# Loading q and k of the first two batches as a casting DMA in 1.5 KB runs, in GpSimd's queue, beside plain loads in SyncE's

## The chip, the cores and the metric

The kernel runs on one core of a Trainium2 chip. The metric is the device time of one execution in microseconds. Five engines run side by side, each through its own queue of instructions in program order: TensorE (PE; its weight loads are the row PEld), VectorE (DVE), ScalarE (ACT), GpSimd (POOL) and SyncE (SP). DMAs are issued from such a queue too; SP issues most of them here, and POOL issues those that change the type on the way. All of them are carried by the same 16 DMA engines.

## The reference

Sliding-window attention with a linear distance bias, followed by one feed-forward layer:

```python
# q, k, v: (8 batches, 8 heads, 576 tokens, 64), float32
scores = q @ k.T / sqrt(64)                      # per batch and head
mask   = (rel >= 0) & (rel < 128)                # rel = query - key
scores = where(mask, scores - slope[h] * abs(rel), -1e9)
attn   = softmax(scores) @ v
x      = attn.transpose(0, 2, 1, 3).reshape(4608, 512)
h      = x @ w_in                                # (512, 2048)
out    = (h * clip(h + 3, 0, 6) / 6) @ w_out     # (2048, 512)
```

## The kernel before

**Attention.** The unit of work is a pair of heads, `g` = 0 to 31: pair `g` belongs to batch `g // 4`. A pair's q and k are needed transposed, with the 64 dimensions on the partitions: two heads fill 128. `scores` (line 186) multiplies blocks of 128 keys by the same block of queries (`scd`) and by the next one (`sco`). `exp_diag` and `exp_off` take the exponential on ACT, and POOL masks the result in place (lines 216, 228, 232). `values` (line 236) multiplies by v, which carries a column of ones for the sums, in two calls, one for three blocks of queries and one for two; DVE divides. `back` (line 264) writes the result transposed into `xT`: on PE and DVE for the last pair and for batches below `NB_PE`, by a transposing DMA (an "xbar") from SP for the others.

**Loading.** q, k and v arrive as float32 in four rotating buffers. A row of `load_tokens` (line 97) brings a batch's q, k or v in five DMAs, one for each block of tokens; every packet is the 256 bytes of one token of one head. Batch 0 comes in the finer order of `load_pair`. From there q and k go one of two ways. In batch 0, `prepare` casts a pair on DVE, and `transposes` turns it on PE, five blocks each for q and k, with copies out of PSUM on DVE and ACT. In all later batches, `cast_tokens` casts the whole batch on POOL into `qbuf` or `kbuf`, and `xbar` (line 156) turns it by one DMA from SP into `qTb` or `kTb`. v is cast on POOL always. The two weights are loaded and cast to bfloat16 by POOL's DMAs, in 2 KB packets, w_in after pair 0 and w_out after pair 7.

**Feed-forward.** `units` (line 318) lists 288 units of four matmuls of 512 columns: `moe_up` (L284, then ACT L288 and DVE L289) and `moe_down` (L301). `fill(n)` writes the next n units into the program, unless the next one is a `moe_up` whose 512 tokens (one "nt") are not all done: `done` counts the pairs whose result is in `xT`. nt 0 needs batch 0, nt 1 needs batch 1, nt 2 needs batch 2.

**Order.** All engines run in the order in which the program is written. `first_batch` does pairs 0 to 3 without units. After it come seven units, and `segment` takes pairs 4 to 31 in loops: scores of `g`, exponentials of `g`, values of `g - 1`, with units between them by a table of seven places (two in a loop of batch 1, eight from batch 2 on). At the end of a loop `stage_next` issues casts, xbars and loads for later batches. So a cast on POOL, which waits for a load or a buffer, stands ahead of the next pair's masks, and an xbar in SP's queue stands behind the loads issued before it.

## Time and profile before

| | us |
|---|---|
| median of 3 runs | 395.62 (395.07 to 396.06) |
| profiled execution | 395.14 |
| its span, first to last instruction | 393.4 |
| PE busy | 311.4 (79%) |
| ACT, DVE, POOL busy | 199.0, 164.3, 151.3 |
| mean granted TensorE clock | 0.939 |

The span is cut into 40 slices of 9.8 us on the page. Views used below are the slices, the list of who waited for whom, the groups of instructions by line, the timeline of one engine, windows of chosen length, and the instructions of one tile. In a timeline a row is start, duration, engine, line, operation, output and inputs, and how many were merged; in square brackets stands the idle time ahead of it and what ended it. `SPq` is SP issuing DMAs.

### The profile page before, as it was taken

The numbers are of one execution on the slowest core, as the hardware profiler recorded it, in microseconds if no ns is written. First come the engines' busy times: TensorE is split into PE (matmuls) and PEld (weight loads), VectorE is DVE, ScalarE is ACT, GpSimd is POOL, SyncE is SP. The second block draws the span as 40 slices with busy tenths as digits, with TensorE's granted clock in tenths as the row PEclk, the third lists the DMA queues.
The fourth block names the chain that finished last, engine by engine and source line by source line (L and its number), as shares of the span: only waits on it lengthen the run. The fifth ranks groups of instructions, "written<-read, shape, count | busy, mean of one in ns | idle before, by whom it ended". The sixth has DMA issues, their size and how long they took to land.

```text
span 393.4 us, 6368 instructions
## 1 busy us (share of the span) xinstructions
PE 311.4 (79%) x2334; PEld 156.3 (40%) x2369; DVE 164.3 (42%) x348; ACT 199.0 (51%) x365; POOL 151.3 (38%) x246
## 2 busy tenths in 40 slices
PE   2577407600458989998999899899999999999985
PEld 1354103300324544554454455454554444444432
DVE  5654402510126534544554455455545544344420
ACT  2653306810327754675776567576677533444410
POOL 1684405980232665555467455536224100000000
PEclk9999957955659999999999999999999999999999
DMA  7999999899994996999699799952121101001012
GB/s 159 219 196 203 200 215 214 153 160 192 202 163 97 223 223 144 205 198 211 148 211 238 131 221 214 220 112 57 48 71 45 46 27 53 28 27 55 27 53 80
DMA packets 176718, 55.95 MB, mean 142 GB/s; under 512 B 167856, under 2 KB 172208, under 8 KB 176688
## 3 DMA queue, kind: packets, MB, share of 16 engines
q1 hardware_dynamic: 172320, 51.23, 69.2%
q0 software_dynamic: 4224, 4.19, 6.7%
q8 instruction: 18, 0.29, 0.3%
q10 hardware_dynamic: 144, 0.13, 0.1%
q14 instruction: 12, 0.10, 0.1%
HBM read 36.70 MB, written 9.44 MB: 117 GB/s over the span
## 4 chain that ended last, share of the span: by engine, by line
PE 59%; SPq 20%; DMA 8%; ACT 3%; issue 3%; POOL 3%; DVE 2%; POOLq 0%
PE ops L301 28%; PE hps L284 25%; SPq L101 14%; DMA xT<-avs 4%; SPq L90 3%; DMA ld_v<-in_v_dram 3%; SPq L158 2%; ACT r L288 2%; PE av L249 2%; PE scd L193 2%; DMA ld_q<-in_q_dram 1%; PE av L246 1%; DVE osb L315 1%; DVE g L289 1%; POOL pd L216 1%
## 5 line engine op out<-in xcount | busy, mean ns | idle before, releaser
L289 DVE SCALAR_TENSOR_TENSOR g<-r,hps 128x512 bf16<-128x512 f32 x144 | 99.0, 688 | 188.0 <-ACT r L288 187.9
L288 ACT ACTIVATE r<-hps,bias 128x512 f32<-128x512 f32 x144 | 99.7, 692 | 140.8 <-PE hps L284 138.5
L284 PE MATMUL hps<-xT,w_in_sb 128*128 128x512 bf16 x552 | 152.4, 393 | 12.5 <-DMA xT<-avs 8.1
L301 PE MATMUL ops<-w_out_sb,g 128*128 128x512 bf16 x565 | 143.6, 379 | 4.4 <-DVE osb L315 3.4
L301 PEld LDWEIGHTS <-g 128*128 128x128 bf16 x576 | 56.2, 98 | 76.4 <-issue 10.3
L216 POOL TENSOR_SCALAR_AFFINE_SELECT pd<-pd 128x512 bf16<-128x512 bf16 x64 | 39.4, 639 | 107.9 <-ACT pd L213 107.9
L284 PEld LDWEIGHTS <-w_in_sb 128*128 128x128 bf16 x576 | 52.4, 100 | 63.9 <-issue 16.8
L228 POOL TENSOR_SCALAR_AFFINE_SELECT po<-po 128x512 bf16<-128x512 bf16 x64 | 40.7, 640 | 26.8 <-ACT po L223 23.4
L213 ACT ACTIVATE pd<-scd,bias_d 128x512 bf16<-128x512 f32 x64 | 41.0, 688 | 18.7 <-PE scd L193 15.5
L223 ACT ACTIVATE po<-sco,bias_o 128x512 bf16<-128x512 f32 x64 | 44.3, 693 | 0.0
L193 PE MATMUL scd<-qTb,kTb 64*128 64x128 bf16 x256 | 14.0, 235 | 37.4 <-DMA kTb<-kbuf 36.0
L246 PE MATMUL av<-vbuf,po 128*128 128x65 bf16 x256 | 25.9, 201 | 8.3 <-DVE avs L255 8.3
L255 DVE TENSOR_TENSOR avs<-av,rc 128x384 bf16<-128x384 f32 x64 | 31.4, 491 | 2.2
L193 PEld LDWEIGHTS <-kTb 64*128 64x128 bf16 x256 | 7.9, 100 | 48.8 <-DMA kTb<-kbuf 36.6
L246 PEld LDWEIGHTS <-po 128*128 128x128 bf16 x256 | 20.4, 103 | 13.4 <-DVE avs L255 10.6
L249 PE MATMUL av<-vbuf,pd 128*128 128x65 bf16 x256 | 25.1, 202 | 0.0
L249 PEld LDWEIGHTS <-pd 128*128 128x128 bf16 x256 | 20.6, 103 | 10.3 <-issue 1.1
L226 ACT ACTIVATE p4buf<-sco,bias_d 128x64 bf16<-128x64 f32 x64 | 20.9, 327 | 0.0
L152 POOL CAST qbuf<-ld_q 128x1024 bf16<-128x1024 f32 (+1 forms) x21 | 18.1, 903 | 3.7 <-DMA ld_q<-in_q_dram 3.7
L152 POOL CAST kbuf<-ld_k 128x1024 bf16<-128x1024 f32 (+1 forms) x21 | 18.1, 896 | 3.7 <-DMA ld_k<-in_k_dram 3.7
L313 ACT COPY osb<-ops 128x512 f32<-128x512 f32 x18 | 10.5, 586 | 16.7 <-PE ops L301 16.7
L200 PE MATMUL sco<-qTb,kTb 64*128 64x128 bf16 (+1 forms) x256 | 12.9, 226 | 4.4 <-ACT p4buf L226 4.4
(49 smaller groups left out, 136.4 us busy)
## 6 DMA issues: line engine op xcount, KB each, us to landing
out_dram<-osb SPq DMA_DIRECT2D x35, 256.0 KB, 2.3
ld_q<-in_q_dram SPq DMA_DIRECT2D x28, 256.0 KB, 4.8
ld_k<-in_k_dram SPq DMA_DIRECT2D x28, 256.0 KB, 5.2
ld_v<-in_v_dram SPq DMA_DIRECT2D x28, 256.0 KB, 5.1
ld_q<-in_q_dram SPq DMA_DIRECT2D x16, 128.0 KB, 3.9
ld_k<-in_k_dram SPq DMA_DIRECT2D x16, 128.0 KB, 4.0
ld_v<-in_v_dram SPq DMA_DIRECT2D x16, 128.0 KB, 4.0
w_in_sb<-in_moe_w_in_dram POOLq DMA_DIRECT2D x4, 512.0 KB, 11.6
```

The costliest lines, as they stand in the source:

```text
L101: nc.sync.dma_start(out=ld[b, nm][:n, j, :, :], in_=src[b, :, ds(j * 128, n), :].rearrange("h p d -> p h d"))
L152: nc.gpsimd.tensor_copy(out=dst[:m, lo:lo + n, :].rearrange("p j c -> p (j c)"), in_=s[:m, lo:lo + n, :, :].rearrange("p j h d -> p (j h d)"))
L213: nc.scalar.activation(out=pd[:, e, :, :].rearrange("p j c -> p (j c)"), in_=sc[:, e, :], func=ACT.Exp, bias=bias_d[:, h:h + 1], scale=scale)
L216: nc.gpsimd.affine_select(out=pd[:, e, :, :], in_=pd[:, e, :, :], pattern=[[0, 4], [1, 128]], channel_multiplier=-1, base=0, compare_op=AL ...
L223: nc.scalar.activation(out=po[:, e, :, :].rearrange("p j c -> p (j c)"), in_=sc[:, e, :], func=ACT.Exp, bias=bias_o[:, h:h + 1], scale=scale)
L228: nc.gpsimd.affine_select(out=po[:, e, :, :], in_=po[:, e, :, :], pattern=[[0, 4], [-1, 128]], channel_multiplier=1, base=-1, compare_op=A ...
L246: nc.tensor.matmul(av[:, i, e, :], lhsT=po[:, e, qt - 1, :], rhs=vb[:, qt - 1, h, :], start=True, stop=False)
L249: nc.tensor.matmul(av[:, i, e, :], lhsT=d, rhs=vb[:, qt, h, :], start=(qt == 0), stop=True)
L284: nc.tensor.matmul(hps, lhsT=w_in_sb[:, ks, ts(ms, 128)], rhs=xT[:, ks, ts(nt, NT)], start=(ks == 0), stop=(ks == n_ks - 1))
L288: nc.scalar.activation(out=r6, in_=hps, func=ACT.Relu, bias=bias3[:, 0:1], scale=1.0 / 6.0)
L289: nc.vector.scalar_tensor_tensor(out=gts[nt][:, ms, :], in0=r6, scalar=1.0, in1=hps, op0=ALU.min, op1=ALU.mult)
L301: nc.tensor.matmul(ops[nt, sub], lhsT=gts[nt][:, ms, ts(sub, 128)], rhs=w_out_sb[:, ms, :], start=(ms == 0), stop=(ms == n_ms - 1))
```

## The change

Batches 0 and 1 take q and k another way. `load_runs` loads them from POOL's queue, cast to bfloat16 in the DMA. A partition holds six neighbouring tokens of a head (96 partitions × 6 = 576), so that a packet reads 1.5 KB; batch 0 comes in eight DMAs, one for each pair and name, batch 1 in two. `prepare` on DVE only reorders a pair, `transposes` does six blocks of 96 for q and k each, and one copy puts the tokens back in order as it leaves PSUM. `NB_PE = 2` sends batch 1 this way, with its transposes in `segment`; its results go back on PE as well, since `by_xbar` begins with pair 8.

The order of issue moves. POOL issues q and k of batch 0 and all of w_in at the start, q and k of batch 1 after pair 0, and w_out after pair 1. SP issues v of batch 0 at once, then v of batch 1, then q and k of batch 2. v of batch 2 comes in the loop of pair 5. `qTb` and `kTb` are laid out by pair, and the later batches' casts go by block into one `tbuf`, which q and k now share. The four load buffers are taken in turn by an explicit list, where q and k of batches 0 and 1 take one buffer together. Three units follow batch 0 instead of seven, and a loop of batch 1 has three instead of two.

```diff
-    NB_PE = 1
+    RP, RT = 96, 6
+    NB_PE = 2
...
-    qbuf = held.tile([128, NQ, H * D], BF16, name="qbuf")
-    kbuf = held.tile([128, NQ, H * D], BF16, name="kbuf")
+    tbuf = held.tile([128, NP, NQ, 128], BF16, name="tbuf")
+    ldbuf = [held.tile([128, (H * RT * D, NQ * H * D)[i % 2]], FP32, name=f"ldbuf{i}")
+             for i in range(4)]
...
-    qTb = [held.tile([128, NQ, NP, 128], BF16, name=f"qTb{i}") for i in range(2)]
-    kTb = [held.tile([128, NQ, NP, 128], BF16, name=f"kTb{i}") for i in range(2)]
+    qTb = [held.tile([128, NP, NQ, 128], BF16, name=f"qTb{i}") for i in range(2)]
+    kTb = [held.tile([128, NP, NQ, 128], BF16, name=f"kTb{i}") for i in range(2)]
...
+    def next_ld():
+        nld[0] += 1
+        return ldbuf[(nld[0] - 1) % 4]
+
+    def new_runs(b):
+        t = next_ld()[:, :].bitcast(BF16)
+        for n, nm in enumerate("qk"):
+            ld[b, nm] = t[:RP, ts(n, H * RT * D)].rearrange("p (h c) -> p h c", h=H)
+
+    def load_runs(b, hs):
+        for nm in "qk":
+            nc.gpsimd.dma_start(
+                out=ld[b, nm][:, hs, :],
+                in_=src_of[nm][b, hs, :, :].rearrange("h (p t) d -> p h (t d)", t=RT))
...
-        dst = qbuf if nm == "q" else kbuf
-        for lo, n, m in ((0, 2, 128), (2, 2, 128), (4, 1, LAST)):
-            nc.gpsimd.tensor_copy(
-                out=dst[:m, lo:lo + n, :].rearrange("p j c -> p (j c)"),
-                in_=s[:m, lo:lo + n, :, :].rearrange("p j h d -> p (j h d)"))
+        for j in range(NQ):
+            m = min(128, S - j * 128)
+            nc.gpsimd.tensor_copy(out=tbuf[:m, :, j, :],
+                                  in_=s[:m, j, :, :].rearrange("p (i e) d -> p i (e d)", e=2))
...
-            pr = prs.tile([128, NQ, 2, D], BF16, tag=f"pr{nm}", name="pr")
-            t = ld[b, nm]
-            nc.vector.tensor_copy(out=pr[:, 0:4, :, :], in_=t[:, 0:4, hs, :])
-            nc.vector.tensor_copy(out=pr[:LAST, 4, :, :], in_=t[:LAST, 4, hs, :])
+            pr = prs.tile([RP, RT, 2, D], BF16, tag=f"pr{nm}", name="pr")
+            nc.vector.tensor_copy(
+                out=pr.rearrange("p t e d -> p e t d"),
+                in_=ld[b, nm][:, hs, :].rearrange("p e (t d) -> p e t d", t=RT))
...
-            for j in range(NQ):
-                n = min(128, S - j * 128)
-                nc.tensor.transpose(tp[:, ds(j * 128, n)], src[:n, j, :], ident[:n, :n])
-            eng = nc.vector.tensor_copy if nm == "q" else nc.scalar.copy
-            eng(out=dst[:, 0:4, hp, :], in_=tp[:, 0:512].rearrange("p (j c) -> p j c", j=4))
-            eng(out=dst[:, 4, hp, 0:LAST], in_=tp[:, 512:S])
+            tp = ps_h.tile([128, RT, RP], BF16, tag="h", name="tp", padded_shape=[128, 8, 128])
+            for t in range(RT):
+                nc.tensor.transpose(tp[:, t, :], src[:, t, :], ident[:RP, :RP])
+            eng = nc.scalar.copy if nm == "k" and g % 2 == 0 else nc.vector.tensor_copy
+            eng(out=dst[:, hp, :, :].rearrange("p j c -> p (j c)")[:, 0:S].rearrange(
+                "p (a t) -> p a t", t=RT), in_=tp.rearrange("p t a -> p a t"))
...
     def by_xbar(g):
-        return XBAR_X and NB_PE * NP <= g < G - 1
+        return XBAR_X and 2 * NP <= g < G - 1
...
         if g == 0:
-            load_weights_in()
-        if g == 2:
-            for nm in "qkv":
-                load_tokens(1, nm, src_of[nm])
+            new_runs(1)
+            load_runs(1, slice(0, H))
+            load_tokens(1, "v")
+        if g == 1:
+            load_weights_out()
         if b == 1:
+            if hp == 1:
+                load_tokens(2, "v")
+            if hp in (1, 2):
+                xbar(2, "qk"[hp - 1])
             if hp < 3:
                 cast_tokens(2, "qkv"[hp])
-            if hp in (1, 2):
-                xbar(2, "qk"[hp - 1])
-            if hp == 3:
-                load_weights_out()
...
+            pe_next = g + 1 < hi and (g + 1) // NP < NB_PE
             if g < hi:
                 scores(g)
             fill(f[0])
             if g < hi:
                 exp_diag(g, 0)
+            if pe_next:
+                transposes(g + 1)
...
+            if g + 2 < hi and (g + 2) // NP < NB_PE:
+                prepare(g + 2)
             fill(f[5])
...
-        for nm in "qkv":
-            new_load(0, nm)
+        new_runs(0)
+        load_tokens(0, "v")
+        constants()
         for hp in range(NP):
-            for nm in "qkv":
-                load_pair(0, nm, src_of[nm], hp)
-                if hp == 0:
-                    load_tail(0, nm, src_of[nm])
-        constants()
+            load_runs(0, slice(2 * hp, 2 * hp + 2))
+        load_weights_in()
         first_batch()
-        for nm in "qkv":
-            cast_tokens(1, nm)
-        xbar(1, "q")
-        load_tokens(2, "q", q)
-        xbar(1, "k")
-        load_tokens(2, "k", k)
-        load_tokens(2, "v", v)
-        fill(7)
-        segment(NP, G, lambda g: (0, 1, 0, 1, 0, 0, 0) if g < 2 * NP else (1, 1, 1, 1, 1, 1, 2))
+        load_tokens(2, "q")
+        load_tokens(2, "k")
+        prepare(NP)
+        transposes(NP)
+        prepare(NP + 1)
+        fill(3)
+        segment(NP, G, lambda g: (1, 0, 1, 0, 1, 0, 0) if g < 2 * NP else (1, 1, 1, 1, 1, 1, 2))
```

The first place that the prediction speaks of is POOL's queue at the start of the program. Before, behind the constants, it reads (`128x4x2x64` is the cast of v for one pair, `x2` two rows alike):

```order
L109 IOTA rel_i 128x1
L138 CAST vbuf_106<-ld_v 128x4x2x64
L139 CAST vbuf_106<-ld_v 64x2x64
L138 CAST vbuf_106<-ld_v 128x4x2x64
L139 CAST vbuf_106<-ld_v 64x2x64
L216 AFFINE_SELECT pd<-pd 128x512 x2
L228 AFFINE_SELECT po<-po 128x512 x2
```

In the changed kernel POOL's queue at the same place, from the last two of the eight DMAs of batch 0, reads:

```order
L97 DMA ldbuf_102<-in_q_dram 96x2x384
L97 DMA ldbuf_102<-in_k_dram 96x2x384
L130 DMA w_in_sb<-in_moe_w_in_dram 128x4x512 x4
L142 CAST vbuf_106<-ldbuf_103 128x4x2x64
L143 CAST vbuf_106<-ldbuf_103 64x2x64
L142 CAST vbuf_106<-ldbuf_103 128x4x2x64
L143 CAST vbuf_106<-ldbuf_103 64x2x64
L218 AFFINE_SELECT pd<-pd 128x512 x2
```

Twelve DMAs now stand ahead of the first cast of v, which waits for SP's load of the whole of v of batch 0 (`ldbuf_103`), where before it waited for a pair's part.

The second place is SP's queue from the loads of batch 2 to the xbar of its k. Before, the loads of q, k and v of batch 2 lie around batch 1's two xbars (`111`, `113`), and those of batch 2 (`110`, `112`) follow with batch 1's results between them:

```order
L158 DMA_TRANSPOSE qTb_111<-qbuf 128x20x128
L101 DMA ld_q<-in_q_dram 128x8x64 x4
L101 DMA ld_q<-in_q_dram 64x8x64
L158 DMA_TRANSPOSE kTb_113<-kbuf 128x20x128
L101 DMA ld_k<-in_k_dram 128x8x64 x4
L101 DMA ld_k<-in_k_dram 64x8x64
L101 DMA ld_v<-in_v_dram 128x8x64 x4
L101 DMA ld_v<-in_v_dram 64x8x64
L268 DMA_TRANSPOSE xT<-avs 128x5x128
L158 DMA_TRANSPOSE qTb_110<-qbuf 128x20x128
```

In the changed kernel SP's queue from q of batch 2 on reads (`ldbuf_104` held q and k of batch 1 before):

```order
L106 DMA ldbuf_102<-in_q_dram 128x8x64 x4
L106 DMA ldbuf_102<-in_q_dram 64x8x64
L106 DMA ldbuf_103<-in_k_dram 128x8x64 x4
L106 DMA ldbuf_103<-in_k_dram 64x8x64
L106 DMA ldbuf_104<-in_v_dram 128x8x64 x4
L106 DMA ldbuf_104<-in_v_dram 64x8x64
L161 DMA_TRANSPOSE qTb_110<-tbuf 128x20x128
L106 DMA ldbuf_105<-in_q_dram 128x8x64 x4
L106 DMA ldbuf_105<-in_q_dram 64x8x64
L161 DMA_TRANSPOSE kTb_112<-tbuf 128x20x128
```

No xbar of batch 1 is left; between the two xbars of batch 2 stands the load of q of batch 3.

The third place is POOL's queue in the loops of pairs 5 and 6 of the changed kernel, from the last cast of v of batch 1 to the cast of v of batch 2 (`ldbuf_103` now holds k of batch 2):

```order
L142 CAST vbuf_107<-ldbuf_105 128x4x2x64
L143 CAST vbuf_107<-ldbuf_105 64x2x64
L156 CAST tbuf<-ldbuf_103 128x4x128 x4
L156 CAST tbuf<-ldbuf_103 64x4x128
L218 AFFINE_SELECT pd<-pd 128x512 x2
L230 AFFINE_SELECT po<-po 128x512 x2
L234 AFFINE_SELECT p4buf_108<-p4buf_108 128x2x64
L149 CAST vbuf_106<-ldbuf_104 128x16x64 x2
```

The cast of k of batch 2 writes `tbuf`, which the xbar of q of batch 2 reads, and the masks of pair 6 stand behind it.

More of the change, by code (lines that the diff above doesn't have):

```diff
@@ L113, in constants @@
             nc.vector.memset(p4buf[i], 1.0)
[L114 to L116 removed]
+            nc.vector.memset(kTb[i][:, :, 4, LAST:128], 0.0)
+        nc.vector.memset(tbuf[64:128, :, 4, :], 0.0)
         nc.vector.tensor_copy(out=rel_f, in_=rel_i)
```

41 lines of the change are left out of this document (13 added, 28 removed).

## The prediction

> **What bounds the kernel now.** I read the page's 40 slices first. Each slice is 9.8 us; a digit is the busy share in tenths.
>
> ```profile
> span 393.4 us, 6368 instructions
> PE   2577407600458989998999899899999999999985
> PEclk9999957955659999999999999999999999999999
> DMA  7999999899994996999699799952121101001012
> ```
>
> PE is nearly full from about 120 us to the end. Before that it has two holes, at slices 5 and 8 to 9, where the granted clock falls to 0.5, and there the DMA row stays at 9. So the first 120 us belong to the DMA and the rest to PE. The list of waits and PE's own timeline name the holes:
>
> ```profile
> PE scd L193 <- DMA kTb<-kbuf: 36.0, 2, 21.7
> ...
> 59.32 0.61 PE L193 MATMUL scd<-qTb,kTb 64*128 64x128 bf16 x8 [14.36 <-DMA kTb<-kbuf]
> 74.47 0.40 PE L193 MATMUL scd<-qTb,kTb 64*128 64x128 bf16 x8
> 101.09 0.61 PE L193 MATMUL scd<-qTb,kTb 64*128 64x128 bf16 x8 [21.68 <-DMA kTb<-kbuf]
> 113.32 2.29 PE L284 MATMUL hps<-xT,w_in_sb 128*128 128x512 bf16 x5 [4.02 <-DMA xT<-avs]
> 124.20 0.40 PE L193 MATMUL scd<-qTb,kTb 64*128 64x128 bf16 x8
> 132.31 0.40 PE L193 MATMUL scd<-qTb,kTb 64*128 64x128 bf16 x8
> ```
>
> Scores of pair 4 (batch 1) start at 59.32 after 14.36 us of waiting for the transposed k, those of pair 8 (batch 2) at 101.09 after 21.68. Pair 10 starts at 124.20, pair 11 at 132.31: 8.1 us a loop from there on, each with 8 MoE units of four 512-column matmuls. Windows over these stretches (columns PE, PEld, DVE, ACT, POOL busy, clock, DMA share, GB/s written):
>
> ```profile
> 6.00:17.00 11.00, 5.70 (x60) 3.84 (x60) 5.47 (x14) 5.40 (x12) 4.85 (x10) 1.00 1.29 215
> 21.00:35.00 14.00, 9.46 (x117) 7.13 (x119) 8.06 (x21) 6.38 (x14) 10.14 (x18) 1.00 1.21 199
> 101.10:124.20 23.10, 15.36 (x107) 7.36 (x108) 7.60 (x16) 10.73 (x20) 7.99 (x13) 0.71 0.87 147
> 124.20:393.00 268.80, 255.54 (x1842) 125.46 (x1871) 122.11 (x233) 151.87 (x272) 93.02 (x149) 1.00 0.62 124
> ```
>
> After 124.20 PE is busy 255.5 of 268.8 us and DMA has room. So the time is "when pair 10 starts" plus about 269 us, and the change is worth what it takes off that start.
>
> **What the transfers cost.** From 6 to 17 us only 256-byte packets move: 215 GB/s. Between 18 and 36 us w_in is beside them:
>
> ```profile
> q1 hardware_dynamic: 172320, 51.23, 69.2%
> q0 software_dynamic: 4224, 4.19, 6.7%
> ...
> 16.82 11.46 SPq L101 DMA_DIRECT2D ld_q<-in_q_dram  x5
> 17.75 3.10 POOL L126 DMA_DIRECT2D w_in_sb<-in_moe_w_in_dram  x4
> 36.59 1.59 POOL L152 CAST qbuf<-ld_q 128x1024 bf16<-128x1024 f32 x2 [3.66 <-DMA ld_q<-in_q_dram]
> ...
> L126 POOL DMA_DIRECT2D w_in_sb<-in_moe_w_in_dram x4: 750/765/878, 17.8 to 20.1; - x4
> ...
> DMA to landing us min/median/max: 7.2/11.6/15.6
> ```
>
> The last two rows are w_in's: first landing at 17.75+7.2 = 25.0, last at about 20.1+15.6 = 35.7, so three pieces of 1.05 MB read take 10.7 us, 3.57 us each: 294 GB/s read. ld_q of batch 1 (8·576·64·4 B = 1.18 MB) shares the engines and is waited for until 36.59, 18.8 us for 1.18 MB: 63 GB/s. Together some 350 GB/s against 215. POOL's queue of large packets goes first in effect, and SP's gets about a fifth.
>
> The 1.5 KB runs are not in this trace. One weight packet of 2 KB takes 2048/(294/16) = 111 ns of an engine in company; a run takes between three quarters of that (by bytes, 83) and all of it (by count, 111). A batch's q and k are 1536 runs, 96 per engine: 8.0 to 10.7 us; I take 9.7, nearer the count.
>
> **The change, step by step.** In the timeline POOL's last constant and DVE's last one stand at:
>
> ```profile
> 1.33 0.13 POOL L109 IOTA rel_i<- 128x1 int32 x1
> 5.42 0.14 DVE L121 TENSOR_SCALAR bias_o<-rel_f 128x1 f32<-128x1 f32 x1
> ```
>
> POOL's queue carries q,k of batch 0 (9.7), w_in (4·3.57 = 14.3), q,k of batch 1 (9.7) and w_out (14.3): 48 us. From 1.5 us I allow 2 us to first data: it ends at 51.5 (bounds 48 to 54).
>
> SP carries v of batches 0 and 1, q and k of batch 2, v of batch 2, q of batch 3: six loads, 7.08 MB. Alone until 3.5 us it moves 0.3 MB, and then 63 GB/s. So **v of batch 0 lands at** 3.5+(1.18−0.30)/0.063 = 17.5 us (bounds: 8 at 215 GB/s throughout, 22 if it has no start). Values need it, and so does POOL, whose first casts of v stand ahead of every mask:
>
> ```profile
> L228 POOL TENSOR_SCALAR_AFFINE_SELECT po<-po 128x512 bf16<-128x512 bf16 x64 | 40.7, 640 | 26.8 <-ACT po L223 23.4
> L232 POOL TENSOR_SCALAR_AFFINE_SELECT p4buf<-p4buf 128x128 bf16<-128x128 bf16 x32 | 9.6, 301 | 0.0
> L138 POOL CAST vbuf<-ld_v 128x512 bf16<-128x512 f32 x4 | 2.8, 695 | 10.7 <-DMA ld_v<-in_v_dram 10.7
> L139 POOL CAST vbuf<-ld_v 64x128 bf16<-64x128 f32 x4 | 1.2, 289 | 0.0
> L152 POOL CAST kbuf<-ld_k 64x512 bf16<-64x512 f32 x7 | 4.3, 608 | 0.0
> ```
>
> A pair's masks cost 4·0.64+0.30 = 2.9, its casts of v 1.0. POOL then runs four pairs of masks (11.6), four of casts (4.0), two issues of runs (768 packets each; by 3.10/4 for 512, 1.2 each, 2.3) and w_out's issue (3.1): 17.5+21 = 38.5 us. Before, this work ended at 31.9:
>
> ```profile
> 31.64 0.29 POOL L232 TENSOR_SCALAR_AFFINE_SELECT p4buf<-p4buf 128x128 bf16<-128x128 bf16 x1
> 34.79 0.40 PE L274 MATMUL tb<-ident,avs 128*128 128x128 bf16 x2 [0.42 <-DVE avs L255]
> 35.40 4.51 PE L284 MATMUL hps<-xT,w_in_sb 128*128 128x512 bf16 x11 [0.22 <-issue]
> ```
>
> So batch 0 gets 6.6 us later, hidden only if batch 1's data set the start anyway: they land at 3.5+9.7+14.3+9.7 = 37.2. From the last masks to the last transposes of batch 0 it is 3.3 us now, so 41.8. Then come copies, transposes and evacuation of pair 4, about 3 (12 transposes of 96 columns for 10, one strided copy out of PSUM for two; unshown, between half and twice as long, 1.5 to 6), and three units on a slow clock at 4.51·4/11 = 1.6 each, partly beside that. **Scores of pair 4 start at 48** instead of 59.3. This first gain is 11 us.
>
> Batch 1's loops now take (74.47−59.32)/3 = 5.05 us with two units; a third unit, 12 q/k transposes and 5 back go in: 6.0 (5 to 7). Reading batch 1's last runs, which frees the buffer for v of batch 2, comes at the end of the second loop: 60. The xbar of q2 stands behind that load:
>
> ```profile
> 62.15 5.80 SPq L101 DMA_DIRECT2D ld_v<-in_v_dram  x5
> 110.66 3.42 SPq L158 DMA_TRANSPOSE qTb<-qbuf  x1
> 228.30 5.13 SPq L101 DMA_DIRECT2D ld_q<-in_q_dram  x5
> DMA to landing us min/median/max: 5.0/5.2/18.7
> ```
>
> Issue of v2 5.5 (65.5). Then the xbar of q2 lands 5.2 after issue and POOL casts k2 into the same tbuf, 5·0.61 = 3.0; beside it SP issues the xbar (3.4) and q3 (5.0): 8.4, the longer. The xbar of k2 lands 5.2 later: 60+5.5+8.4+5.2 = **79 for the scores of pair 8**, instead of 101.1. By bytes: at 51.5 SP has moved 0.3+48·0.063 = 3.3 MB; the other 3.8 MB at 215 GB/s take 17.6, two xbars 6.8 and a landing 2: 78. Both chains agree, so shortening one alone brings little.
>
> From 101.09 to 124.20 lie two loops, 23.1 us, at clock 0.71 and with the 4.02 us wait for an xbar of batch 1's output. That wait goes, since PE transposes that batch: pair 8's loop can take 4 units for 1. At 8.1 us per 8 units and 0.87 per unit, the loops are 4.6 and 8.1; for the slow clock after a hole I add 3: 16, so pair 10 starts at 95. There POOL waits for the next xbar of q, behind 10 loads of k3 and v3, ahead of pair 9's masks: 2 (0 to 8). So 97, a gain of 27.2, and 27 units done instead of 24: 3·0.87 = 2.6, of which 2.2 counts, since the third nt lacks tokens until batch 2 is through. End: 393.4−27.2−2.2 = 364.0, plus 395.14−393.4 = 1.7 around the span: **366 us**. The profiled execution (395.14) lies 0.5 below the median of the three runs (395.62), less than matters here.
>
> In the later batches one tbuf for q and k makes POOL's cast of k wait for q's xbar:
>
> ```profile
> 214.86 0.29 POOL L232 TENSOR_SCALAR_AFFINE_SELECT p4buf<-p4buf 128x128 bf16<-128x128 bf16 x1
> 215.56 4.69 SPq L158 DMA_TRANSPOSE qTb<-qbuf  x1
> 228.55 0.23 PE L249 MATMUL av<-vbuf,pd 128*128 128x65 bf16 x2
> ```
>
> With a landing at 215.56+5.2 = 220.8, the cast (3.0) and the two pd masks (1.3) end at 225.1; PE reads them at 228.55. It costs nothing with 3.4 us of cover.
>
> [...]
>
> **Rivals.**
> - *More overlap*: runs cost their bytes only (8.0), SP's share rises, pair 4 and pair 10 come 5 to 8 us earlier: 358. For it: 83 ns by bytes. Against: POOL's chain from v of batch 0.
> - *SP starves or the xbars queue*: if SP moves nothing while POOL's queue is full, its 6.8 MB start at 51.5: +31.6+8.8 = 92, 13 later: 379. For it: SP's fifth above and a k xbar of 18.7 us behind loads and w_out. Against: w_out is gone by then.
> [...]
> - *No gain*: POOL's queue moves only 215 GB/s read (13.1 MB, 61 us) and SP starves: 3.5+61+31.6+8.8 = 105, about the 101 of now: 395. Against: 294 GB/s measured.
> - *Slower*: POOL's wait for q's xbar in each of batches 2 to 6, if the landing takes the 18.7 of the worst row: 215.56+18.7+4.3 = 238.6 against 228.55, 10 us, five times: 366+50 = 416. It eats the whole gain of 29 from a landing of 8.7+29/5 = 14.5 us on. Against: the median of 5.2.
>
> **How the numbers follow.** Forecast 366: 0.50. More overlap, 358: 0.10. Starving, 379: 0.20. Late descriptors, 369: 0.05. No gain, 395: 0.05. Slower, 416: 0.10. The range takes the first four with the bounds of runs, loops and copies, 354 to 384. Faster by over 0.3% (what a measurement here can tell from no change) is 0.85, within it 0.05, slower 0.10.
>
> **What would show it.** PE's scores of pairs 4, 8 and 10 at 48, 79 and 97, and the granted clock's hole shorter. POOL's first cast of v waiting until 17.5. POOL's queue landing its last weights near 52. POOL idle ahead of the cast of k2, released by q's xbar. After pair 13 loops of 8.1 us again, without waits for masks. The prediction is wrong if POOL's queue moves far from 294 GB/s, if SP's share isn't near a fifth, or if PE waits for masks each batch.

## The result, and the profile after

The changed kernel takes **375.10 us** (median of 4 runs, 374.02 to 375.62) beside 395.44 of the kernel before on the same chip: a ratio of 0.948 with a 95% interval of 0.9456 to 0.9505, 5% faster. The profiled execution took 375.08, its span 373.4. Forecast were 366 and a range of 354 to 384. The page of after, its span, PE's slices, the granted clock and the DMA's (a slice is now 9.3 us):

```profile
span 373.4 us, 6509 instructions
PE   1456765666998699979999999999999999999995
PEclk9999996969999989999999999999999999999999
DMA  9999997999399959995998999531131010010012
```

PE's empty slices 5, 8 and 9 of before are gone; it works at five to seven tenths from slice 2 on, and is nearly full from slice 10 on instead of 12, but for slice 13. The clock still falls at slices 6 and 8, and a little at 14. Scores of pairs 4, 8, 10, 12, 13 and 14 in PE's timeline:

```profile
46.19 0.40 PE L195 MATMUL scd<-qTb,kTb 64*128 64x128 bf16 x8
83.08 0.40 PE L195 MATMUL scd<-qTb,kTb 64*128 64x128 bf16 x8
101.85 0.34 PE L195 MATMUL scd<-qTb,kTb 64*128 64x128 bf16 x6
120.13 0.40 PE L195 MATMUL scd<-qTb,kTb 64*128 64x128 bf16 x8
126.49 0.40 PE L195 MATMUL scd<-qTb,kTb 64*128 64x128 bf16 x8
138.82 0.40 PE L195 MATMUL scd<-qTb,kTb 64*128 64x128 bf16 x8
```

Pair 4 starts 13.1 us earlier than before, pair 8 18.0, pair 10 22.4, and at the end 20.0 are left. So batch 1 hands on more than it gained at its start, and after pair 10 something is given back. Of a gain forecast as 29 us, 20 came. The rest of the document follows these facts.

The table holds every kernel run, cut at the scores of pairs 4, 8 and 14. The starts are from PE's timeline of its profiled execution, the last column is span less the start of pair 14; ratios are to the kernel before on the same chip, with 95% intervals. They leave out four executions in a slower state, one each of e_prep6_act and e_back_pe and two of e_lead_even, the profiled one among these two.

| kernel | median us | ratio | pair 4 at | 4 to 8 | 8 to 14 | 14 to end |
|---|---|---|---|---|---|---|
| before | 395.44 | 1 | 59.3 | 41.8 | 56.9 | 235.4 |
| after | 375.10 | 0.948 (0.9456 to 0.9505) | 46.2 | 36.9 | 55.7 | 234.6 |
| e_packets256 | 390.77 | 0.9876 (0.9842 to 0.991) | 61.8 | 36.7 | 55.7 | 234.0 |
| e_before_wout | 392.38 | 0.9938 (0.9904 to 0.9972) | 69.8 | 28.9 | 57.9 | 234.6 |
| e_win_later | 379.67 | 0.9621 (0.9574 to 0.9667) | 50.2 | 37.3 | 55.2 | 234.3 |
| e_two_tbuf | 374.59 | 0.9468 (0.9415 to 0.9521) | 44.4 | 38.2 | 57.6 | 232.9 |
| e_prep6_act | 371.24 | 0.9371 (0.9332 to 0.9409) | 44.1 | 34.4 | 56.9 | 232.7 |
| e_two_act67 | 368.90 | 0.9349 (0.9305 to 0.9394) | 44.0 | 33.7 | 55.7 | 233.3 |
| e_xbar_first | 366.66 | 0.9278 (0.9234 to 0.9323) | 43.8 | 29.2 | 58.2 | 234.4 |
| e_units7 | 372.86 | 0.9412 (0.9364 to 0.9461) | 44.2 | 36.3 | 53.5 | 236.2 |
| e_back_pe | 379.53 | 0.9639 (0.9578 to 0.97) | 42.5 | 36.1 | 55.1 | 241.0 |
| e_down_lead | 377.54 | 0.9552 (0.9498 to 0.9607) | 44.6 | 37.0 | 56.7 | 237.6 |
| e_first_and_lead | 372.23 | 0.944 (0.9384 to 0.9496) | 46.5 | 29.9 | 56.0 | 237.6 |
| e_lead_even | 364.48 | 0.9217 (0.9168 to 0.9266) | 46.3 | 29.9 | 57.1 | 232.8 |

One caution for reading it: after, e_units7, e_down_lead and e_back_pe are alike as far as pair 4, and it starts there between 42.5 and 46.2. A pair's absolute start is worth little below 3 us; stretches and the ratios of whole runs are what the verdicts rest on.

### The profile page after: what moved, and what is told of

Read it like the earlier page. It is cut to its first block, busy times and chain, and to the rows that moved or that the text cites. A ratio compares the mean times of both kernels' runs of the same rounds, so it can differ in the third digit from the quotient of the medians.

```text
span 373.4 us, 6509 instructions
## 1 busy us (share of the span) xinstructions
PE 315.8 (85%) x2408; PEld 160.3 (43%) x2445; DVE 174.2 (47%) x355; ACT 198.5 (53%) x361; POOL 155.3 (42%) x279
## 3 DMA queue, kind: packets, MB, share of 16 engines
q0 software_dynamic: 7456, 6.55, 10.8%
## 4 chain that ended last, share of the span: by engine, by line
PE 62%; DVE 8%; ACT 8%; issue 7%; POOL 7%; DMA 6%; SPq 1%; another core or an unknown queue 0%; POOLq 0%
PE ops L303 28%; PE hps L286 28%; ACT r L290 4%; DVE g L291 3%; DMA ldbuf<-in_v_dram 3%; DMA xT<-avs 3%; POOL pd L218 2%; ACT po L225 2%; PE av L251 2%; PE av L248 2%; PE scd L195 2%; POOL po L230 2%; DVE avs L257 1%; DVE osb L317 1%; PE sco L202 1%
## 5 line engine op out<-in xcount | busy, mean ns | idle before, releaser
L291 DVE SCALAR_TENSOR_TENSOR g<-r,hps 128x512 bf16<-128x512 f32 x144 | 99.1, 688 | 146.5 <-ACT r L290 146.4
L303 PEld LDWEIGHTS <-g 128*128 128x128 bf16 x576 | 55.7, 98 | 78.0 <-issue 13.9
L156 POOL CAST tbuf<-ldbuf 128x512 bf16<-128x512 f32 (+1 forms) x60 | 34.0, 610 | 43.1 <-issue 36.2
L225 ACT ACTIVATE po<-sco,bias_o 128x512 bf16<-128x512 f32 x64 | 44.1, 690 | 0.0
L248 PE MATMUL av<-vbuf,po 128*128 128x65 bf16 x256 | 27.1, 203 | 8.2 <-DVE avs L257 6.2
L251 PE MATMUL av<-vbuf,pd 128*128 128x65 bf16 x256 | 27.0, 205 | 7.2 <-POOL pd L218 7.2
L251 PEld LDWEIGHTS <-pd 128*128 128x128 bf16 x256 | 21.2, 104 | 17.6 <-POOL pd L218 8.2
L256 DVE RECIPROCAL rc<-av 128x6 f32<-128x6 f32 x64 | 11.8, 184 | 23.6 <-PE av L251 23.4
L183 PE MATMUL tp<-ident,pr 96*128 96x96 bf16 x96 | 8.8, 255 | 16.1 <-DVE pr L171 10.4
L315 ACT COPY osb<-ops 128x512 f32<-128x512 f32 x18 | 10.5, 585 | 19.3 <-PE ops L303 19.3
L317 DVE COPY osb<-ops 128x512 f32<-128x512 f32 x17 | 11.6, 684 | 7.4 <-PE ops L303 7.4
L195 PE MATMUL scd<-qTb,kTb 64*128 64x128 bf16 x256 | 13.6, 229 | 1.8 <-DVE kTb L185 1.0
```

Source lines behind the costliest of these rows:

```text
L156: nc.gpsimd.tensor_copy(out=tbuf[:m, :, j, :], in_=s[:m, j, :, :].rearrange("p (i e) d -> p i (e d)", e=2))
L225: nc.scalar.activation(out=po[:, e, :, :].rearrange("p j c -> p (j c)"), in_=sc[:, e, :], func=ACT.Exp, bias=bias_o[:, h:h + 1], scale=scale)
L248: nc.tensor.matmul(av[:, i, e, :], lhsT=po[:, e, qt - 1, :], rhs=vb[:, qt - 1, h, :], start=True, stop=False)
L251: nc.tensor.matmul(av[:, i, e, :], lhsT=d, rhs=vb[:, qt, h, :], start=(qt == 0), stop=True)
L291: nc.vector.scalar_tensor_tensor(out=gts[nt][:, ms, :], in0=r6, scalar=1.0, in1=hps, op0=ALU.min, op1=ALU.mult)
L303: nc.tensor.matmul(ops[nt, sub], lhsT=gts[nt][:, ms, ts(sub, 128)], rhs=w_out_sb[:, ms, :], start=(ms == 0), stop=(ms == n_ms - 1))
```

## The experiments

### Where the gain comes from

**e_packets256** keeps the change's queues and order, but a partition takes one token from each of six blocks of 96 instead of six neighbours, so that a packet reads 256 bytes again. The copy out of PSUM puts the tokens in order to match.

```diff
-                out=ld[b, nm][:, hs, :],
-                in_=src_of[nm][b, hs, :, :].rearrange("h (p t) d -> p h (t d)", t=RT))
+                out=ld[b, nm][:, hs, :].rearrange("p h (t d) -> p h t d", t=RT),
+                in_=src_of[nm][b, hs, :, :].rearrange("h (t p) d -> p h t d", t=RT))
...
-                "p (a t) -> p a t", t=RT), in_=tp.rearrange("p t a -> p a t"))
+                "p (t a) -> p t a", t=RT), in_=tp)
```

> q and k of batches 0 and 1 stay casting DMAs in GpSimd's queue, at the same places and with the same bytes, but every packet is one token of one head again (256 bytes read) instead of six (1.5 KB). Theory that the packets' size buys the gain: a batch's q and k are 9216 packets, 576 per engine, at some 40 ns each in company (215 GB/s is 19 ns per 256-byte packet, and SyncE's queue takes its turn) 23 us instead of 9.7. Twice 13 us more ahead of batch 1: scores of pair 4 near 70 instead of 46.2, pair 8 near 100, time 388 to 400. Rival that the second queue and the order of issue buy it: time stays at 375, within 3.

The lines of the two pages for POOL's queue (packets, MB, share of 16 engines' span), and the instructions of the run loads (ns min/median/max; issue to landing in us), first of after:

```profile
q0 software_dynamic: 7456, 6.55, 10.8%
L97 POOL DMA_DIRECT2D ldbuf<-in_q_dram x5: 637/657/789, 1.6 to 22.4; - x5
DMA to landing us min/median/max: 5.1/7.8/13.5
```

and of e_packets256:

```profile
q0 software_dynamic: 22816, 6.55, 15.7%
L97 POOL DMA_DIRECT2D ldbuf<-in_q_dram x5: 869/872/1800, 1.6 to 21.2; - x5
DMA to landing us min/median/max: 6.5/13.0/32.9
```

The same 6.55 MB take 0.157·388.1 = 60.9 us of 16 engines instead of 0.108·373.4 = 40.3, and the slowest of the ten loads, k of batch 1, lands 32.9 us after its issue instead of 13.5. Pair 4 falls back to 61.8, later than before the change, and all of the loss lies ahead of it: the other three stretches are those of after. The ratio goes from 0.948 to 0.9876: the packet's size is worth about 0.04·395 = 15.7 us of the gain of 20, and all the rest of the change together, with 256-byte packets, about 5.

**e_before_wout** is the kernel before with one part of the change alone: w_out is loaded in the loop of pair 1 instead of pair 7.

```diff
+        if g == 1:
+            load_weights_out()
...
-            if hp == 3:
-                load_weights_out()
```

> The kernel before with one part of the change alone: the load of w_out moves from the loop of pair 7 to the loop of pair 1. No bytes go away. Theory (the first hole is a matter of how 256-byte packets and large packets share the engines): w_out's 14 us in POOL's queue now run beside batch 1's q, k, v, so pair 4 starts later, 63 to 70 instead of 59.3; batch 2's k no longer lies beside w_out, so its hole shrinks from 21.7 by as much, and pair 8 starts at 97 to 102. Time within 390 to 397, no gain of 20. Rival (w_out's place is what the change gained by): pair 8 starts before 90 and the time is 375 to 385.

Its scores of pairs 4 and 8 in PE's timeline:

```profile
69.84 0.61 PE L193 MATMUL scd<-qTb,kTb 64*128 64x128 bf16 x8 [23.75 <-DMA kTb<-kbuf]
98.70 0.61 PE L193 MATMUL scd<-qTb,kTb 64*128 64x128 bf16 x8 [7.88 <-DMA kTb<-kbuf]
```

As the theory had it, pair 4 starts 10.5 us later than before, since the wait ahead of it grows from 14.36 to 23.75, and the wait of pair 8 shrinks from 21.68 to 7.88. Pair 8 starts 2.4 us earlier, and the ratio of 0.9938 is 2.4 us too. Where a weight stands in the queue moves a hole; it hardly fills it.

**e_win_later** issues w_in after pair 0 instead of at the start, ahead of batch 1's runs.

```diff
         if g == 0:
+            load_weights_in()
             new_runs(1)
...
-        load_weights_in()
         first_batch()
```

> The four loads of w_in are issued after pair 0, ahead of q and k of batch 1, instead of at the start; all the rest as in the changed kernel. Theory that v of batch 0 is late (17.9) because GpSimd's queue takes four fifths of the engines: q and k of batch 0 are through near 12, then SyncE's queue is alone, v of batch 0 lands at 13 to 14, GpSimd's work of batch 0 ends 3 to 4 us earlier; but GpSimd's queue stands empty for some us, w_in, q and k of batch 1 and w_out land as much later: pair 4 at 46 to 49, time 374 to 378. Rival that v of batch 0 sets the start of batch 1: pair 4 at 42 to 43, time 371 to 372.

v of batch 0, with less beside it, lets POOL cast from 14.48 to 16.1 instead of 14.65 to 19.0, but its masks of batch 0 end at 35.7 all the same: the issue of w_in, 3.00 us of POOL's time, now stands between the masks of pairs 0 and 1. Batch 1's last runs land 21.2 us after issue instead of 13.5, behind w_in. The copies on DVE that reorder q and k of pair 4 read, in after and then (the second of two) in e_win_later:

```profile
39.76 0.61 DVE L171 COPY pr<-ldbuf 96x768 bf16<-96x768 bf16 x2
```

```profile
44.44 0.36 DVE L171 COPY pr<-ldbuf 96x768 bf16<-96x768 bf16 x1 [3.65 <-DMA ldbuf<-in_k_dram]
```

In after they come right behind the copy of batch 0's last result (39.38 to 39.84) and wait for no DMA, since the runs landed at 23.1+13.5 = 36.6: there the end of batch 0's work sets the start of batch 1. In e_win_later they wait 3.65 us for k, and the runs set it. Pair 4 starts at 50.2 and the run takes 379.7, both later than theory and rival expected; by the ratios, 0.9621 instead of 0.948, that is 5.6 us more than after. The run shows that w_in behind pair 0 costs more than it brings. What an earlier end of batch 0 would be worth it doesn't show, since POOL's work of batch 0 ended no earlier.

### The loops of batch 1

Pair 4 was 1.8 us earlier than forecast, and pair 8 4.1 later. Here is the loop of pair 5 in after, from the timelines of DVE, POOL and PE around the copies that reorder q and k of pair 6, with two such copies at another time (41.53) in the first row.

```profile
41.53 0.62 DVE L171 COPY pr<-ldbuf 96x768 bf16<-96x768 bf16 x2
...
54.48 3.50 DVE L171 COPY pr<-ldbuf 96x768 bf16<-96x768 bf16 x2
54.93 2.84 POOL L156 CAST tbuf<-ldbuf 128x512 bf16<-128x512 f32 x5
57.90 0.67 DVE L291 SCALAR_TENSOR_TENSOR g<-r,hps 128x512 bf16<-128x512 f32 x1
58.62 0.64 PE L183 MATMUL tp<-ident,pr 96*128 96x96 bf16 x6 [3.31 <-DVE g L291]
```

Two copies that took 0.62 us at 41.53 take 3.50 at 54.48: they end at 57.98, 0.2 us after the last of POOL's five casts of q2. Behind them wait the activation of a MoE unit (L291) and, for that, PE's transposes. POOL's casts, 0.57 each, are no slower for it (2.84 for five, as at 73.05 below). Later in the same batch (timelines of SP, POOL and PE of after) POOL waits for the one `tbuf`, and SP issues one thing after the other:

```profile
56.85 10.57 SPq L106 DMA_DIRECT2D ldbuf<-in_v_dram  x5
67.52 3.88 SPq L161 DMA_TRANSPOSE qTb<-tbuf  x1
71.50 4.35 SPq L106 DMA_DIRECT2D ldbuf<-in_q_dram  x5
73.05 2.84 POOL L156 CAST tbuf<-ldbuf 128x512 bf16<-128x512 f32 x5 [7.70 <-issue]
75.95 3.71 SPq L161 DMA_TRANSPOSE kTb<-tbuf  x1
76.53 0.24 PE L251 MATMUL av<-vbuf,pd 128*128 128x65 bf16 x1 [2.49 <-POOL pd L218]
```

The issue of v2 holds SP until 67.42, since its last DMAs need the buffer that pair 7's copies free. The xbar of q2 comes after it, the cast of k2 waits 7.70 us for it, and PE 2.49 for the masks behind that cast.

**e_prep6_act** takes pair 6's two reordering copies from DVE to ACT.

```diff
-            nc.vector.tensor_copy(
+            eng = nc.scalar.copy if g == NP + 2 else nc.vector.tensor_copy
+            eng(
```

> The two reordering copies of pair 6 alone go from VectorE to ScalarE. [...]

If the one copy of 3.23 us is what lengthens the loop of pair 5, that loop was to fall from 12.0 to 9 us and the time to 371.5 to 373; if the chain of PSUM buffers is, the loop was to stay at 12 or grow, with 375 to 376. The same place in this kernel, on ACT and POOL:

```profile
51.63 1.57 ACT L172 COPY pr<-ldbuf 96x768 bf16<-96x768 bf16 x2
52.67 2.84 POOL L156 CAST tbuf<-ldbuf 128x512 bf16<-128x512 f32 x5
```

ACT's two copies take 1.57 us and end beside the casts, which take 2.84 as before. The loop of pair 5 falls from 12.0 to 8.8 us, and its granted clock rises from 0.72 to 1.00: the 3.2 us hold the stall and the slow clock behind it. The stretch from pair 4 to 8 is 2.5 us shorter. The ratio goes from 0.948 to 0.9371, 4.3 us, with intervals apart; what it has over the 2.5 lies in stretches that the edit does not touch.

Two kernels that are like after in this place show the stall at other sizes without any edit there, because q2's last pieces landed later in them and broke up POOL's row of casts. Beside five casts in a row (2.84 us, after) the two copies take 3.50, beside four (2.40, e_units7) 2.38, beside three (1.85, e_back_pe) 1.82, and the loop of pair 5 takes 12.02, 11.12 and 9.14.

**e_two_tbuf** gives q and k a buffer each (and `prs` one buffer in place of two, for room).

```diff
-    tbuf = held.tile([128, NP, NQ, 128], BF16, name="tbuf")
+    tbufs = {nm: held.tile([128, NP, NQ, 128], BF16, name="tbuf" + nm) for nm in "qk"}
```

> q and k of the later batches get a buffer each again ahead of their xbars; to make room the reordered pairs have one buffer instead of two. Theory that the shared buffer costs: GpSimd's waits of 7.7 us ahead of k of batch 2 and of 6.9 us ahead of k of batch 3 are gone, TensorE's loop of pair 7 falls from 11.4 to about 8 us, but scores of pair 8 then wait for the xbar of k, which SyncE issues behind q of batch 3 (about 76, landed 81): pair 8 at 81 instead of 83.1, time 371 to 373. Rival that the wait is covered by the load of q of batch 3 and the masks: 375, within 0.5.

The expected 3 us did not come. POOL no longer waits, but the cast of k2 now runs at another time, and the same thing happens to the next pair's copies too (timelines of POOL, DVE, SP and PE of this kernel):

```profile
63.53 2.96 POOL L157 CAST tbufk<-ldbuf 128x512 bf16<-128x512 f32 x5
63.62 3.10 DVE L172 COPY pr<-ldbuf 96x768 bf16<-96x768 bf16 x2
68.04 3.72 SPq L162 DMA_TRANSPOSE qTb<-tbufq  x1
71.85 4.60 SPq L106 DMA_DIRECT2D ldbuf<-in_q_dram  x5
76.56 3.71 SPq L162 DMA_TRANSPOSE kTb<-tbufk  x1
82.65 0.61 PE L196 MATMUL scd<-qTb,kTb 64*128 64x128 bf16 x8 [3.93 <-DMA kTb<-tbufk]
```

Pair 6's copies are as long as before, and the loop of pair 5 is 12.02 again. Now pair 7's are long as well, the loop of pair 6 takes 10.2 instead of 7.9, and they are again as long as the casts beside them; a copy that reads PSUM, at 67.24 beside POOL's masks, keeps its 0.74. And although k2 is cast by 66.5, its xbar is issued at 76.56, behind q2's and the load of q3, and pair 8 waits 3.93 us for it. The wait was taken from POOL, and stands in SP's queue.

**e_two_act67** joins the two and moves pair 7's copies to ACT as well.

```diff
+            eng = nc.scalar.copy if g in (NP + 2, NP + 3) else nc.vector.tensor_copy
```

> A buffer each for q and k ahead of their xbars, and the reordering copies of pairs 6 and 7 on ScalarE: both GpSimd's wait for the xbar and VectorE's long copies beside GpSimd's casts should be gone. Theory that the one hid behind the other when each was taken away alone: loops of pairs 5, 6 and 7 at 8 to 9 us each, pair 7 no longer waits for masks, pair 8 then waits for the xbar of k, which SyncE issues behind q of batch 3, 14.5 to 15 us after the last issue of v of batch 2: pair 8 at 76 to 78, time 366 to 369. Rival that moving the copies did all there is: as with the copies of pair 6 alone, pair 8 at 78 to 79, time 370 to 371.5.

Time (368.9) and the start of pair 8 (77.6) are as expected, the loops are not: those of pairs 5 and 7 take 10.36 and 10.21 instead of 8 to 9. The first has no long copy, but a granted clock of 0.69, whose cause was not followed up; in the last, pair 8 waits 3.75 us for k's xbar, which is SP's order. Against e_prep6_act (0.9371) the intervals overlap widely, so that what the second buffer and pair 7's copies add is not settled.

**e_xbar_first** changes that on top: in batch 1's first two loops q2 and k2 are cast and turned, and only then the loads of v2 and q3 are issued; v2 is cast one loop later.

```diff
         if b == 1:
+            if hp < 2:
+                cast_tokens(2, "qk"[hp])
+                xbar(2, "qk"[hp])
             if hp == 1:
                 load_tokens(2, "v")
-            if hp in (1, 2):
-                xbar(2, "qk"[hp - 1])
-            if hp < 3:
-                cast_tokens(2, "qkv"[hp])
+            if hp == 3:
+                cast_tokens(2, "v")
```

> As the kernel with two buffers and the copies of pairs 6 and 7 on ScalarE, and SyncE issues the xbars of q and k of batch 2 right behind their casts, ahead of v of batch 2 and q of batch 3; GpSimd's cast of v of batch 2 moves behind the masks of pair 7. Theory that the load of v stands in the xbars' way: xbar of q near 56, of k near 64, so pair 8 waits for neither; it starts when four loops of batch 1 are through, 44 to 46 plus 30: 74 to 76, time 364 to 367. Rival that the loops of batch 1 set pair 8 anyway: same as without the new order, within 1 us.

Pair 4 to 8 takes 29.2 instead of 33.7, less than the 31 that were forecast for the change itself. Of these 4.4 us only 2 to 3 arrive at the end (0.9349 to 0.9278, with intervals that overlap a little): 8 to 14 grows by 2.5, where loop 13 now takes 13.6.

### After pair 10

Loops 12 and 13 of after: rows of SP's and PE's timeline, and two windows (columns as in the prediction):

```profile
127.72 1.28 SPq L270 DMA_TRANSPOSE xT<-avs  x1
130.26 0.38 PE L286 MATMUL hps<-xT,w_in_sb 128*128 128x512 bf16 x1 [2.39 <-DMA xT<-avs]
127.36:130.77 3.41, 1.02 (x5) 0.38 (x5) 0.00 (x0) 0.10 (x1) 0.00 (x0) 1.00 0.68 198
130.77:134.18 3.41, 3.23 (x18) 1.51 (x18) 1.44 (x3) 1.75 (x3) 0.05 (x1) 0.50 0.87 165
```

The units are three ahead, so in loop 12 only five are left that do not need the third nt's tokens, and it takes 6.36 us. Loop 13 begins with the first `moe_up` of that nt, which waits 2.39 us for the xbar of pair 11's output; and behind the wait the clock is at 0.50 for 3.41 us. Loop 13 takes 12.33.

**e_units7** has seven units in place of eight in the loops of pairs 9 to 11, to have some left for loop 12.

```diff
+                (1, 1, 1, 1, 1, 1, 1) if 2 * NP < g < 3 * NP else (1, 1, 1, 1, 1, 1, 2))
```

> Seven units instead of eight in each loop of pairs 9, 10 and 11, so that pair 12 starts with 40 units done as in the kernel before. Theory that running three units ahead was lost and cost more: the loop of pair 12 has eight units and 8 to 9 us instead of five and 6.4, the loop of pair 13 goes from 12.3 to 8 to 9 us without the 2.4 us wait for an xbar of the output, loops 9 to 11 are 0.9 to 1.4 us shorter each; pair 14 starts 3 to 4 us earlier, time 371 to 372.5. Rival that the order of units doesn't matter while TensorE is full: 375, within 0.5.

From 8 to 14 it takes 53.5 instead of 55.7, but from 14 to the end 236.2 instead of 234.6: 0.6 of 2.2 us stay. The waits on `xT` did not go, against the theory: they are 5.2 us in four as in after, and loop 13 takes 10.3. In the run itself it is 0.7% faster than after, with intervals that overlap by 0.0005. Unclear, and no way to keep the lead.

**e_back_pe** sends the last pair of each batch back through PE and DVE, and not by an xbar.

```diff
-        return XBAR_X and 2 * NP <= g < G - 1
+        return XBAR_X and 2 * NP <= g < G - 1 and g % NP != NP - 1
```

> The changed kernel, but the result of the last pair of each batch goes back by TensorE and VectorE instead of an xbar (30 more transposes, 6 copies of 0.45 us). Theory that TensorE's waits for that xbar at the next batch's first unit (5.2 us in four waits, the first of 2.4 us followed by 3.7 us at a granted clock of 0.56) are what ate the lead after pair 10: the waits are gone, the loop of pair 13 falls from 12.3 to 8 to 9 us, no low clock after it, time 367 to 370. Rival that they only move to another wait: 374 to 376.

It was slower than after, against the theory. The waits for `xT` are gone, but the added transposes and copies wait for DVE, and a batch's four loops take 35.4 us (8.46 + 8.95 + 8.46 + 9.53) instead of the 33.4 that after needs on average: 14 to the end is 6.5 us longer.

**e_down_lead** is to let three `moe_down` units of the nt before stand ahead, so that loop 12 has eight units.

```diff
+    LEAD = 3
...
-        for step in range(16):
-            if nt < n_nt:
-                units.append((nt, moe_up, step))
-            units.append((nt, moe_down, step))
+        for step in range(16 + LEAD):
+            if step < 16:
+                units.append((nt, moe_down, step))
+            if nt < n_nt and step >= LEAD:
+                units.append((nt, moe_up, step - LEAD))
```

> The changed kernel with each nt from the third on beginning with three moe_down units ahead of its first moe_up. Theory (the lead in units is lost since the first moe_up after a batch waits for the xbar of its output, and the granted clock drops behind that wait): the waits on xT fall from 5.2 us to under 1, loop 13 from 12.3 to about 9, pair 14 starts 2 to 3 us earlier, 368 to 373. Rival (the units are only moved about, the short loop ahead of it pays): pair 14 within 1 us of 138.8, 374 to 376.

**e_first_and_lead** does the same on top of e_xbar_first.

> The best kernel so far (two transposed buffers for q and k, ACT copies of pairs 6 and 7, xbars of batch 2 ahead of the next loads; 366.7) with the same three moe_down units ahead. There pair 13's loop was 13.6 us with a 3.7 us wait on xT. Theory: that wait and the low clock behind it go, 360 to 364. Rival (the lead comes back as idle time elsewhere): 366 to 367.

Neither gained: e_first_and_lead is slower than e_xbar_first, with intervals apart, and e_down_lead is 0.7% above after, with intervals that overlap a little. The waits on `xT` vanish and the clock stays at 1.00 there, but from pair 14 on every loop is 8.5 to 8.8 us instead of 8.11. Waits of PE on DVE's division of the attention output (sum, times, longest), e_xbar_first and then e_first_and_lead:

```profile
PE av L250 <- DVE avs L259: 7.3, 9, 1.9
```

```profile
PE av L250 <- DVE avs L259: 11.9, 24, 1.9
```

With `LEAD = 3` four `moe_down` stand ahead, not three, since the step that brings the first `moe_up` puts a `moe_down` before it. The odd unit shifts the whole order: a loop begins with a `moe_down` where it began with a `moe_up`, and the activations of `moe_up` (ACT L292, DVE L293) come between the masks' exponentials and the division at another point. That this is what PE then waits for is argued from the list. **e_lead_even** is e_first_and_lead with a lead of two, hence three `moe_down`, and `moe_up` first again.

```diff
-    LEAD = 3
+    LEAD = 2
```

> The kernel of e_first_and_lead with a lead of two instead of three, so that three moe_down units stand ahead of a first moe_up, and not four, and loop 13 begins with a moe_up as in the changed kernel. In e_first_and_lead the waits on xT were gone and the clock stayed at 1.00, yet a batch's loops took 34.6 us instead of 33 since each loop began with a moe_down and the masks' exponentials came at another place among ACT's work. Theory (the order of up and down within a loop is what took the gain back, not the lead): loops of 8.1 us again from pair 14 on, pair 14 at 127 to 129.5 instead of 131.1, three units more done by then, 360 to 364. Rival (a lead costs what it brings, whatever its parity): loops over 8.4, 366 to 372.

In e_lead_even the same line reads as in e_xbar_first again, 7.3 us in nine waits, and one wait of 1.5 on `xT` is left.

One unit more or less changes the ratio from 0.944 to 0.9217, 8.8 us. A batch's loops now take 33.2 us (8.12 + 8.34 + 8.11 + 8.67) instead of 34.6 (8.66 + 8.46 + 8.66 + 8.79), much the same as after's 33.4: between what the theory (8.1) and the rival (over 8.4) expected, and pair 14, at 133.3, was later than 129.5. The profiled execution took 367.8, 3.3 above the median of 364.5, and began batch 1 2.6 later than that of e_xbar_first, so its absolute starts say little. This is the fastest kernel of the study, 10 us faster than the change; against e_xbar_first (0.9278) the intervals overlap, so that the 2.4 us between them, what the lead itself would be worth, are not settled.

## Why the prediction was right, and what it mis-sized

**Right: the queues.** POOL's queue was forecast to land its last weights at 51.5; the issues of w_out and their landings read:

```profile
L136 POOL DMA_DIRECT2D w_out_sb<-in_moe_w_out_dram x4: 752/765/776, 27.5 to 29.8; - x4
DMA to landing us min/median/max: 12.4/16.3/20.6
```

29.8+20.6 = 50.4. v of batch 0 was forecast for 17.5, and three rows of POOL's timeline read:

```profile
17.93 0.29 POOL L143 CAST vbuf<-ldbuf 64x128 bf16<-64x128 f32 x1 [2.66 <-DMA ldbuf<-in_v_dram]
23.14 0.77 POOL L97 DMA_DIRECT2D ldbuf<-in_k_dram  x1
35.47 0.28 POOL L234 TENSOR_SCALAR_AFFINE_SELECT p4buf<-p4buf 128x128 bf16<-128x128 bf16 x1
```

The cast of v's last block waits until 17.93. The last runs of batch 1 land at 36.6 (forecast 37.2), and POOL ends batch 0 at 35.8 (forecast 38.5; an issue of runs costs 0.77, not 1.2). Pair 4 at 46.2 stands 1.8 before the forecast of 48. The rates of 294 and 63 GB/s, taken from one place of the old trace, carried this part: from 1.5 to 50.4 us SP's queue wrote 3.01 MB, 62 GB/s. But 63 is a mean. Where both queues are full, as from 36 to 48 us of after, POOL's queue and SP's moved (packets, MB written, share of 16 engines):

```profile
q0 software_dynamic: 1868, 1.86, 91.2%
q1 hardware_dynamic: 1869, 0.47, 29.8%
```

The packets are equal in number and differ in size; from 36 to 42 us they are 938 and 937, from 42 to 48 us 930 and 932. SP's 256-byte packets thus get 0.47 MB in 12 us, 39 GB/s, and the rest of its 63 comes from the time in which POOL's queue isn't full. e_packets256 shows that the reason given for the rates, the packet's size, was the right one: the same 6.55 MB take 60.9 us of 16 engines instead of 40.3.

**Mis-sized: the loops of batch 1**, "6.0 (5 to 7)". They took 5.58, 12.02, 7.86 and 11.43. What the sum had counted (a unit, 12 transposes, five going back) fits the first. The third is beyond its bound of 7, and takes 7.5 to 7.9 in every kernel with the change in which no copy stalls there. The sum left out what the reordering copies meet on DVE: e_prep6_act takes 3.2 us off the second loop by moving two copies to ACT, and e_two_tbuf gets a second stall where it moves casts beside pair 7's copies. The buffer for v2 thus came free at 66 instead of 60. The chain behind it was right in its order, v2's issue, xbar, cast, q3, xbar, and even shorter than the 19 us forecast. But in after its end does not hold PE: k2's xbar landed at 75.95+5.4 = 81.4, and pair 8 took it up at 83.1 without a wait. PE was held by its middle, the masks behind k2's cast (2.49) and a granted clock of 0.50 from 76.15 to 82.98. e_xbar_first, which takes v2 and q3 out of the chain, makes the stretch 4.4 us shorter, of which 2 to 3 arrive at the end. "Shortening one alone brings little" was wrong: the count by bytes that gave 78 as well had v2 and q3 in it, for which the xbars of batch 2 need not wait.

**Right in sum, not in its terms: pairs 8 to 10**, 18.8 us forecast as 16 + 2. The two loops were to take 4.6 and 8.1, a slow clock 3, and a wait of POOL 2. They took 9.12 and 9.65 at a granted clock of 1.00; in the first PE waits 3.6 us for DVE. POOL did wait 6.86 us for the next xbar of q, but PE waited for no masks behind it. That the sum came out is luck.

**Wrong in sign: the lead of three units.** It was to bring 2.2 us after pair 10; that part took 373.4−101.85 = 271.55 us against 269.2 before, so it cost 2.4, 4.6 from the forecast. Loop by loop, 10 to 12 take 24.6 us for 21 units where before took 25.7 for 24, so that three units, 2.6 us by their price, save 1.0 there; PE waits 1.9 us for output copies in these loops instead of 1.1. Loop 13 is 4.2 longer, 2.39 of it the wait for `xT` and 1.7 a dip of the clock (last section), and from pair 14 on 0.8 come back. The prediction even named the reason, "the third nt lacks tokens until batch 2 is through", but drew the consequence only for the units themselves. A lead that meets a gate ends ahead of it: a short loop, then a first `moe_up` that waits for an xbar whose result nobody had needed so soon. Three tries to keep it, e_units7, e_back_pe and e_down_lead, gave it back elsewhere; e_lead_even may have kept some.

The errors are 4.1 at pair 8, 0.8 to pair 10 and 4.6 after it: with 364.0, the span of 373.4. The 4.1 at pair 8 would be 5.9 if pair 4 had not come 1.8 early.

**The rivals.** More overlap (358) did not come. SP did not starve: pair 8 came at 83, not 92. The slower case had its mechanism right and its price wrong: POOL does wait for q's xbar in the later batches, as the list of waits shows (sum, times, longest):

```profile
POOL tbuf L156 <- issue: 36.2, 5, 8.3
PE av L251 <- POOL pd L218: 7.2, 4, 4.0
```

Of the 36.2 us on POOL little reaches PE: of its 7.2, 4.4 are two waits in batch 0, at 19.66 and 20.25, behind the casts of v, and 2.8 are pair 7's; from pair 8 on PE's waits for masks come to 0.2. The landing that this rival needed, 14.5 us, did not come (5.2 in the median), and e_two_tbuf, which takes POOL's wait away, is no faster. *Late descriptors* (369), a late start of POOL's queue, was the author's estimate: no run shows its 3 us. In after POOL issued its first load of runs at 1.61 us, and the queue moved 5 packets from 3 to 4 us and 134 from 4 to 5, while DVE's constants ran until 5.29; the issues of runs took 637 to 789 ns. What did cost time was DVE's copies beside POOL's casts: a copy of 0.345 us took 3.23 at most, about the time of five casts (2.84) and not of one, and less where the row of casts was shorter.

## What to carry to other kernels

Where 256-byte packets fill the DMA, the run length of a few early loads can be worth more than their order: here 15.7 us, against 2.4 for an earlier w_out and a loss for a later w_in. Rates measured in company in the old trace carried over, but only as the mean of the stretch they came from. When work moves to another engine or time, ask of each copy which engine's row of work it will run beside, and of each lead at which gate it will stop. Before counting a wait as removed, read the queue that issues the next step: here (e_two_tbuf) the wait went from POOL to SP and the time stayed.
